# Longer contiguous runs for the weight loads, fewer K/V DMAs, and two alignment pads in a load-bound decode kernel

## Chip, cores, metric

One core of one Trainium2 chip. The metric is device time in microseconds of a whole launch. A profile's span is some 2 us shorter than the time of the same run, because it counts from the first instruction to the last. A run's state is "fast" or "slow" (over 1.5% above the fastest run of the same kernel); comparisons use fast runs alone.

## The reference

One token (B = S = 1) goes through a windowed attention over a cache and, in parallel, a squared-ReLU MLP. D = 512, 32 heads of 128, window W = 1024, F = 1376; everything is bf16.

```python
xn = layernorm(x)                                   # [1, 512]
q  = xn @ wq                                        # wq [512, 4096]
p  = softmax(q_h . K_h[3072:4096] / sqrt(128))      # per head, 1024 keys
o  = p @ V_h[3072:4096]                             # per head, 128
attn = concat(o) @ wo                               # wo [4096, 512]
mlp  = relu(xn @ w1 + b1)**2 @ w2 + b2              # w1 [512, 1376], w2 [1376, 512]
out  = x + attn + mlp
```

K and V are 8 MB each, wq and wo 4 MB each, w1 and w2 1.4 MB each: 28 MB are read once for very little arithmetic.

## The kernel before

All loads but three small rows (x and the two biases, which ACT issues) are issued by SP in one list, in the order in which they are used. The parts that the change touches (cuts are marked):

```python
plan = []
for kt in range(NKT):                                # wq: 4 DMAs, runs of 8192 B
    plan.append((wq_v[:, kt, :], A_wq[kt*128:(kt+1)*128, :], s_wq, ...))
plan.append((w1_sb, B_w1.rearrange("(k p) n -> p k n", p=128), s_w12, ...))       # runs of 2752 B
plan.append((w2_sb[:, 0:NJ-1, :], B_w2[0:1280].rearrange("(j p) n -> p j n", p=128), ...))  # 1024 B
plan.append((w2_sb[0:96, NJ-1, :], B_w2[1280:F, :], s_w12, ...))
for h in range(HQ):                                  # K: 32 DMAs of 256 KB, runs of 2048 B
    plan.append((k_sb[:, h, :], A_k_cache[0, h, S0:SK, :].rearrange("(p t) d -> p (t d)", p=128), kq[h//HPG], ...))
# ... V likewise, 32 DMAs ...
for g in range(NWO):                                 # wo: 8 DMAs, runs of 1024 B
    plan.append((wo_v[:, 4*g:4*g+4, :], A_wo[...].rearrange("(h d) n -> d h n", d=DH), woq[g], ...))
# PE, end of the kernel
for h in range(HQ):                                  # PV: 256 matmuls, one output column each
    if h % HPG == 0: pe.wait_ge(vq[h // HPG], 16 * HPG)
    # ... 8 matmuls into ot_ps[:, h]
pe.wait_ge(s_ot, 1)                                  # ACT has copied ot_ps to ot_sb
for h in range(HQ):                                  # 128 matmuls into four output columns
    if h % hpg == 0: pe.wait_ge(woq[h // hpg], 16)
    for c in range(4):
        pe.matmul(fin[c], lhsT=wo_v[:, h, c*128:(c+1)*128], rhs=ot_sb[:, h:h+1], ...)
# ... four copies, one transpose, one copy, output DMA
```

Buffers are laid out in SBUF in the order of their declaration. That put wbuf, which holds wq and later wo, 160 B past a multiple of 256 B in each partition, and w1 and w2 likewise.

## Time and profile before

| | before |
|---|---|
| time, median of 4 runs first, of 16 later | 80.44 us, 80.38 us |
| span of the profiled run | 78.2 us |
| DMA packets, bytes | 15,975, 28.1 MB |
| last wo load landed | 75.13 us |

The lines themselves are in the prediction. To read them: the GB/s row has forty slices of 1.96 us; the list of loads and the rates in the slices tell which load is running. "Packets" are what one of the 16 DMA engines moves at a time, one contiguous run each, and the small ones of 4 B are the semaphore writes that end each DMA (1,272 of them before, 16 for each of SP's 79 loads and a few more).

### The profile page before, as it was taken

The numbers are of one execution on the slowest core, as the hardware profiler recorded it, in microseconds if no ns is written. First come the engines' busy times: TensorE is split into PE (matmuls) and PEld (weight loads), VectorE is DVE, ScalarE is ACT, GpSimd is POOL, SyncE is SP. The second block draws the span as 40 slices with busy tenths as digits, with TensorE's granted clock in tenths as the row PEclk, the third lists the DMA queues.
The fourth block names the chain that finished last, engine by engine and source line by source line (L and its number), as shares of the span: only waits on it lengthen the run. The fifth ranks groups of instructions, "written<-read, shape, count | busy, mean of one in ns | idle before, by whom it ended". The sixth has DMA issues, their size and how long they took to land.

```text
span 78.2 us, 2026 instructions
## 1 busy us (share of the span) xinstructions
PE 50.0 (64%) x812; PEld 34.8 (45%) x812; DVE 26.0 (33%) x214; ACT 26.9 (34%) x33; POOL 2.2 (3%) x10
## 2 busy tenths in 40 slices
PE   0000102999296099999999999993398954850940
PEld 0000001358295094445554455371288954850920
DVE  0005500000103999899959990006300000000010
ACT  0501700242000049579999999900600000100011
POOL 7400000000000000000000000000000000000000
PEclk9999999999555555599999999999955555555555
DMA  2799999999999999999999999999999999999700
GB/s 34 285 404 423 431 427 398 400 362 347 368 399 402 405 407 404 400 404 407 401 401 406 406 404 398 410 398 404 402 409 404 395 375 354 350 349 349 233 15 1
DMA packets 15975, 28.12 MB, mean 359 GB/s; under 512 B 1275, under 2 KB 6749, under 8 KB 15454
## 3 DMA queue, kind: packets, MB, share of 16 engines
q1 hardware_dynamic: 15952, 27.99, 96.1%
q8 instruction: 6, 0.10, 0.5%
q14 instruction: 3, 0.02, 0.1%
q10 hardware_dynamic: 14, 0.01, 0.0%
HBM read 27.99 MB, written 0.00 MB: 358 GB/s over the span
## 4 chain that ended last, share of the span: by engine, by line
SPq 79%; DMA 11%; issue 5%; PE 1%; ACT 1%
SPq L227 79%; DMA wbuf<-in_A_wo_dram 11%; PE s_all L568 0%; PE stg L577 0%; ACT orow L301 0%; ACT col_bf L299 0%; PE f_ps L568 0%; PE a_ps L568 0%
## 5 line engine op out<-in xcount | busy, mean ns | idle before, releaser
L284 ACT ACTIVATE kt_sb<-stg 128x1024 bf16<-128x1024 bf16 x20 | 20.3, 1024 | 12.7 <-PE stg L501 11.8
L362 DVE SCALAR_TENSOR_TENSOR junk<-k_sb,qb_sb 128x128 bf16<-128x128 bf16 x96 | 20.6, 285 | 1.2 <-DMA k_sb<-in_A_k_cache_dram 1.2
L501 PE MATMUL stg<-identb,k_sb 128*128 128x128 bf16 x160 | 13.8, 240 | 2.6 <-DMA k_sb<-in_A_k_cache_dram 2.6
L501 PEld LDWEIGHTS stg<-identb,k_sb 128*128 128x128 bf16 x160 | 10.6, 108 | 10.7 <-ACT kt_sb L284 5.5
L508 PE MATMUL s_all<-kt_sb,qmask 128*32 128x512 bf16 x40 | 12.8, 408 | 0.1
L554 PE MATMUL b_ps<-pt_sb,v_sb 128*128 128x1 bf16 x256 | 7.1, 165 | 2.2 <-issue 1.8
L554 PEld LDWEIGHTS b_ps<-pt_sb,v_sb 128*128 128x128 bf16 x256 | 7.0, 104 | 2.4 <-issue 1.9
L362 DVE DVE_READ_ACCUMULATOR junk<-k_sb,qb_sb 128x1 f32 x96 | 7.8, 81 | 0.0
L419 PE MATMUL s_all<-wbuf,xb 128*128 128x512 bf16 x12 | 4.2, 521 | 4.4 <-DMA wbuf<-in_A_wq_dram 4.4
L403 DVE CAST col_bf<-a_ps 128x1 bf16<-128x1 f32 x1 | 0.2, 161 | 16.9 <-PE f_ps L568 16.9
L410 PE MATMUL a_ps<-identb,rows_a 1*128 1x1 bf16 x4 | 0.2, 160 | 8.6 <-DVE rows_a L327 8.6
L568 PE MATMUL a_ps<-ot_sb,wbuf 128*128 128x1 bf16 x32 | 3.6, 165 | 2.7 <-issue 2.7
L568 PEld LDWEIGHTS f_ps<-ot_sb,wbuf 128*128 128x128 bf16 x32 | 3.3, 104 | 2.8 <-issue 2.8
L568 PE MATMUL s_all<-ot_sb,wbuf 128*128 128x1 bf16 x64 | 3.8, 166 | 1.1 <-DMA wbuf<-in_A_wo_dram 0.8
L419 PEld LDWEIGHTS s_all<-wbuf,xb 128*128 128x128 bf16 x12 | 1.4, 126 | 6.8 <-DMA wbuf<-in_A_wq_dram 4.5
L296 ACT ACTIVATE ot_sb<-b_ps 128x32 bf16<-128x32 f32 x1 | 0.2, 198 | 11.9 <-PE b_ps L554 11.9
L274 ACT ACTIVATE qb_sb<-s_all 128x512 bf16<-128x512 f32 x3 | 1.8, 597 | 7.0 <-PE s_all L419 7.0
L443 PE MATMUL b_ps<-xncol,w_sb 128*128 128x1 bf16 (+1 forms) x44 | 3.1, 175 | 1.6 <-DMA w_sb<-in_B_w_dram 1.6
L568 PEld LDWEIGHTS s_all<-ot_sb,wbuf 128*128 128x128 bf16 x64 | 3.5, 105 | 1.4 <-DMA wbuf<-in_A_wo_dram 0.8
L410 PEld LDWEIGHTS a_ps<-identb,rows_a 1*128 1x128 bf16 x4 | 0.2, 100 | 8.5 <-issue 8.5
L337 DVE TENSOR_SCALAR qmask<-a_ps 128x4 bf16<-128x4 f32 x5 | 0.4, 167 | 10.0 <-PE a_ps L430 10.0
L568 PE MATMUL f_ps<-ot_sb,wbuf 128*128 128x1 bf16 x32 | 3.6, 165 | 0.0
(65 smaller groups left out, 37.9 us busy)
## 6 DMA issues: line engine op xcount, KB each, us to landing
k_sb<-in_A_k_cache_dram SPq DMA_DIRECT2D x32, 256.0 KB, 8.5
v_sb<-in_A_v_cache_dram SPq DMA_DIRECT2D x32, 256.0 KB, 8.5
wbuf<-in_A_wq_dram SPq DMA_DIRECT2D x4, 1024.0 KB, 8.0
wbuf<-in_A_wo_dram SPq DMA_DIRECT2D x8, 512.0 KB, 9.5
w_sb<-in_B_w_dram SPq DMA_DIRECT2D x1, 1376.0 KB, 13.9
w_sb<-in_B_w_dram SPq DMA_DIRECT2D x1, 1280.0 KB, 17.2
w_sb<-in_B_w_dram SPq DMA_DIRECT2D x1, 96.0 KB, 16.9
rows_a<-in_A_x_dram ACTq DMA_DIRECT2D x1, 1.0 KB
```

The source lines that it names most:

```text
L227: eng.dma_start(dst, srcap).then_inc(s_, 16)
L274: act.activation(out=qb_sb[:, c * 512 : (c + 1) * 512], in_=s_ps[c % NB_QB][:, :], func=ACT.Copy).then_inc(s_qbev, 1)
L284: act.activation(out=kt_sb[:, i % NS_KT, :], in_=stg_bf[i % NB_STG][:, :], func=ACT.Copy).then_inc(s_evA, 1)
L337: v.tensor_scalar(diag, qt_ps[:, h0 : h0 + 4], inv_sqrt_dh, None, op0=ALU.mult).then_inc(s_qmask, 1)
L362: v.scalar_tensor_tensor(out=junk[:, n % NJUNK, :], in0=k_sb[:, h, t * DH : (t + 1) * DH], scalar=inv_sqrt_dh, in1=qb_sb[:, (4 * ci + j) * ...
L410: ins = pe.matmul(xc_ps[:, kt : kt + 1], lhsT=xn_row[0:1, kt * 128 : (kt + 1) * 128], rhs=one11, start=True, stop=True)
L419: ins = pe.matmul(s_ps[c % NB_QB][:, :], lhsT=xb[:, kt, :], rhs=wq_v[:, kt, b * 512 : (b + 1) * 512], start=(kt == 0), stop=(kt == NKT - 1),)
L443: pe.matmul(ht_ps[0:msz, j : j + 1], lhsT=w1_sb[:, kt, j * 128 : j * 128 + msz], rhs=xncol[:, kt : kt + 1], start=(kt == 0), stop=False,)
L501: ins = pe.transpose(bank[:, t * 128 : (t + 1) * 128], k_sb[:, h, t * DH : (t + 1) * DH], identb[:, :])
L508: ins = pe.matmul(s_ps[c][0:32, :], lhsT=qmask[:, h, :], rhs=kt_sb[:, i % NS_KT, c * 512 : (c + 1) * 512], start=(first_op[c] == (idx, c)) ...
L554: ins = pe.matmul(ot_ps[:, h : h + 1], lhsT=v_sb[:, h, t * DH : (t + 1) * DH], rhs=pt_sb[:, t, h : h + 1], start=(t == 0), stop=(t == NT - 1),
L568: ins = pe.matmul(fin[c], lhsT=wo_v[:, h, c * 128 : (c + 1) * 128], rhs=ot_sb[:, h : h + 1], start=(DEBUG_ATTN_ONLY and h == 0), stop=(h = ...
```

## The change

Its intent is to make each contiguous run longer. A matrix of R rows over 128 partitions is loaded as "partition p takes rows p*k to p*k+k-1" instead of "partition p takes rows p, 128+p, ...", so that k rows are one run. What multiplies the matrix must then be ordered in the same way. For wq and w1 that is a stepped read of the normalised row; for w2 it is a stepped read of w1's columns (step of 10 elements); for wo the attention output, which has one head per column, must be rearranged, which the string of transposes, a permutation matmul and two copies does. K and V go out four heads per DMA. Two pads move the buffers.

```diff
+        pad_w = sb("pad_w", [128, 176], BF16)          # ahead of wbuf
+        pad_k = sb("pad_k", [128, 144], BF16)          # ahead of k_sb
-        for kt in range(NKT):
-            plan.append((wq_v[:, kt, :], A_wq[kt * 128 : (kt + 1) * 128, :], s_wq, ...))
+        plan.append((wbuf[:, :], A_wq.rearrange("(p k) n -> p (k n)", k=NKT), s_wq, ...))      # 32 KB runs
+        plan.append((w1_sb..., B_w1.rearrange("(p k) n -> p (k n)", k=NKT), s_w12, ...))       # 11008 B
+        plan.append((w2a_sb..., B_w2[0:1280].rearrange("(p a) n -> p (a n)", a=NA2), ...))     # 10 KB
+        plan.append((w2b_sb[:, :], B_w2[1280:F, :], s_w12, ...))
+        for g in range(NG):                                # K, V: four heads per DMA, runs still 2 KB
+            plan.append((k_sb[:, hs, :], A_k_cache[0, hs, S0:SK, :].rearrange("h (p t) d -> p h (t d)", p=128), kq[g], ...))
-  "(h d) n -> d h n"
+  wo_src = A_wo.rearrange("(p a) n -> p a n", a=32)        # 4 of 32 rows per DMA: 4 KB runs
     # ... FFN1
-    lhsT=w1_sb[:, kt, j * 128 : j * 128 + msz]
+    lhsT=w1_sb[:, kt, j : j + 10 * 127 + 1 : 10]           # j < 10
     # ... between PV and the wo product
+    for b4 in range(4):
+        pe.transpose(z_ps[rs, :], ot_sb[rs, :], identb[rs, rs], tile_position=(32 * b4, 32 * b4))
+    # VectorE: z_sb <- z_ps
+    pe.matmul(c_ps, lhsT=p4[:, :], rhs=z_sb[:, :], start=True, stop=True)
+    # VectorE: c_sb <- c_ps
-    rhs=ot_sb[:, h : h + 1]
+    rhs=c_sb[:, a : a + 1]
```

(Cut: semaphores, the building of the permutation p4 on GpSimd, the renamed w2 buffers.)

More of the change, by code (lines that the diff above doesn't have):

```diff
@@ L21 @@
 NJ = (F + 127) // 128
+NA2 = 10
+F2T = F - NA2 * 128
 NT = W // 128
@@ L34 @@
 HPG = HQ // NG
+KSEM = 16
 NWO = int(os.environ.get("KDEV_NWO", "8"))
@@ L94, in bass_parallel_sum__sliding_block_cached__dense_activation_squared_relu__decode_kernel @@
         xb = sb("xb", [128, NKT, 128], BF16)
+        pad_w = sb("pad_w", [128, 176], BF16)
         wbuf = sb("wbuf", [128, NKT * HQ * DH], BF16)
         w1_sb = sb("w1_sb", [128, NKT, F], BF16)
-        w2_sb = sb("w2_sb", [128, NJ, D], BF16)
+        w2a_sb = sb("w2a_sb", [128, NA2, D], BF16)
+        w2b_sb = sb("w2b_sb", [F2T, D], BF16)
+        p4 = sb("p4", [128, 128], BF16)
+        z_sb = sb("z_sb", [128, 32], BF16)
+        c_sb = sb("c_sb", [128, 32], BF16)
         hrelu = sb("hrelu", [128, NJ], F32)
@@ L117, in bass_parallel_sum__sliding_block_cached__dense_activation_squared_relu__decode_kernel @@
         wq_v = wbuf[:, :].rearrange("p (k n) -> p k n", k=NKT)
-        wo_v = wbuf[:, :].rearrange("p (h n) -> p h n", h=HQ)
+        wo_v = wbuf[:, :].rearrange("p (a n) -> p a n", a=32)
         one11 = identb[0:1, 0:1]
@@ L134, in bass_parallel_sum__sliding_block_cached__dense_activation_squared_relu__decode_kernel @@
         row4_ps = stg_bf[0][0:4, 256:384]
+        z_ps = stg_bf[1][:, 0:32]
+        c_ps = b_ps[:, 96:128]
         NB_QB = 2
@@ L175, in bass_parallel_sum__sliding_block_cached__dense_activation_squared_relu__decode_kernel @@
         s_colc = sem("s_colc")
+        s_p4 = sem("s_p4")
+        s_zt = sem("s_zt")
+        s_zsb = sem("s_zsb")
+        s_cps = sem("s_cps")
+        s_csb = sem("s_csb")
         s_row4 = sem("s_row4")
@@ L191, in bass_parallel_sum__sliding_block_cached__dense_activation_squared_relu__decode_kernel @@
         plan = []
-        for kt in range(NKT):
-            plan.append((wq_v[:, kt, :], A_wq[kt * 128 : (kt + 1) * 128, :], s_wq, 128 * 4096 * 2, False))
-        plan.append((w1_sb[:, :, :], B_w1.rearrange("(k p) n -> p k n", p=128), s_w12, D * F * 2, False))
-        plan.append((w2_sb[:, 0 : NJ - 1, :], B_w2[0 : (NJ - 1) * 128, :].rearrange("(j p) n -> p j n", p=128), s_w12, 1280 * D * 2, False))
-        plan.append((w2_sb[0 : F - (NJ - 1) * 128, NJ - 1, :], B_w2[(NJ - 1) * 128 : F, :], s_w12, 96 * D * 2, False))
-        for h in range(HQ):
-            plan.append((k_sb[:, h, :], A_k_cache[0, h, S0:SK, :].rearrange("(p t) d -> p (t d)", p=128), kq[h // HPG], W * DH * 2, False))
-        for h in range(HQ):
-            plan.append((v_sb[:, h, :], A_v_cache[0, h, S0:SK, :].rearrange("(p t) d -> p (t d)", p=128), vq[h // HPG], W * DH * 2, False))
-        hpg_ = HQ // NWO
+        plan.append((wbuf[:, :], A_wq.rearrange("(p k) n -> p (k n)", k=NKT), s_wq, D * HQ * DH * 2, False))
+        plan.append((w1_sb[:, :, :].rearrange("p k n -> p (k n)"), B_w1.rearrange("(p k) n -> p (k n)", k=NKT), s_w12, D * F * 2, False))
+        plan.append((w2a_sb[:, :, :].rearrange("p a n -> p (a n)"), B_w2[0 : NA2 * 128, :].rearrange("(p a) n -> p (a n)", a=NA2), s_w12, NA2 * 128 * D * 2, False))
+        plan.append((w2b_sb[:, :], B_w2[NA2 * 128 : F, :], s_w12, F2T * D * 2, False))
+        for g in range(NG):
+            hs = slice(g * HPG, (g + 1) * HPG)
+            plan.append(
+                (
+                    k_sb[:, hs, :],
+                    A_k_cache[0, hs, S0:SK, :].rearrange("h (p t) d -> p h (t d)", p=128),
+                    kq[g],
+                    HPG * W * DH * 2,
+                    False,
+                )
+            )
+        for g in range(NG):
+            hs = slice(g * HPG, (g + 1) * HPG)
+            plan.append(
+                (
+                    v_sb[:, hs, :],
+                    A_v_cache[0, hs, S0:SK, :].rearrange("h (p t) d -> p h (t d)", p=128),
+                    vq[g],
+                    HPG * W * DH * 2,
+                    False,
+                )
+            )
+        apg_ = 32 // NWO
+        wo_src = A_wo.rearrange("(p a) n -> p a n", a=32)
         for g in range(NWO):
@@ L204, in bass_parallel_sum__sliding_block_cached__dense_activation_squared_relu__decode_kernel @@
                 (
-                    wo_v[:, g * hpg_ : (g + 1) * hpg_, :],
-                    A_wo[g * hpg_ * DH : (g + 1) * hpg_ * DH, :].rearrange("(h d) n -> d h n", d=DH),
+                    wo_v[:, g * apg_ : (g + 1) * apg_, :].rearrange("p a n -> p (a n)"),
+                    wo_src[:, g * apg_ : (g + 1) * apg_, :].rearrange("p a n -> p (a n)"),
                     woq[g],
-                    hpg_ * DH * D * 2,
+                    apg_ * 128 * D * 2,
                     True,
@@ L258, in _ @@
                 ).then_inc(s_ident, 1)
+                g.memset(p4[:, :], 0.0).then_inc(s_pool, 1)
+                g.wait_ge(s_pool, 3)
+                p4v = p4[:, :].rearrange("q (a b) -> q a b", b=4)
+                g.affine_select(
+                    out=p4v,
+                    in_=p4v,
+                    compare_op=ALU.not_equal,
+                    fill=1.0,
+                    base=0,
+                    pattern=[[-1, 32], [-32, 4]],
+                    channel_multiplier=1,
+                ).then_inc(s_p4, 1)
             @block.scalar
@@ L353, in d_block @@
                     ci = dblk_index[b]
-                    v.wait_ge(kq[b], 16 * HPG)
+                    v.wait_ge(kq[b], KSEM)
                     v.wait_ge(s_qbev, ci + 1)
@@ L400, in _ @@
                 v.tensor_copy(pt_sb[:, :, :], pt_ps).then_inc(s_ptsb, 1)
+                v.wait_ge(s_zt, 1)
+                v.tensor_copy(z_sb[:, :], z_ps).then_inc(s_zsb, 1)
+                v.wait_ge(s_cps, 1)
+                v.tensor_copy(c_sb[:, :], c_ps).then_inc(s_csb, 1)
                 v.wait_ge(s_final, 1)
@@ L409, in _ @@
                 for kt in range(NKT):
-                    ins = pe.matmul(xc_ps[:, kt : kt + 1], lhsT=xn_row[0:1, kt * 128 : (kt + 1) * 128], rhs=one11, start=True, stop=True)
+                    ins = pe.matmul(xc_ps[:, kt : kt + 1], lhsT=xn_row[0:1, kt : kt + 4 * 127 + 1 : 4], rhs=one11, start=True, stop=True)
                 ins.then_inc(s_xc, 1)
-                pe.wait_ge(s_wq, 16 * NKT)
+                pe.wait_ge(s_wq, 16)
                 if NDB > 0:
@@ L440, in _ @@
                 for j in range(NJ):
-                    msz = min(128, F - j * 128)
+                    if j < NA2:
+                        msz = 128
+                        colsel = slice(j, j + NA2 * 127 + 1, NA2)
+                    else:
+                        msz = F2T
+                        colsel = slice(NA2 * 128, F)
                     for kt in range(NKT):
@@ L444, in _ @@
                             ht_ps[0:msz, j : j + 1],
-                            lhsT=w1_sb[:, kt, j * 128 : j * 128 + msz],
+                            lhsT=w1_sb[:, kt, colsel],
                             rhs=xncol[:, kt : kt + 1],
@@ L449, in _ @@
                         )
-                    ins = pe.matmul(ht_ps[0:msz, j : j + 1], lhsT=b1_row[0:1, j * 128 : j * 128 + msz], rhs=one11, start=False, stop=True)
+                    ins = pe.matmul(ht_ps[0:msz, j : j + 1], lhsT=b1_row[0:1, colsel], rhs=one11, start=False, stop=True)
                 ins.then_inc(s_ht, 1)
@@ L460, in emit_ffn2 @@
                             pe.matmul(fin[c], lhsT=b2_row[0:1, cs], rhs=one11, start=False, stop=False)
-                            for j in range(NJ):
-                                msz = min(128, F - j * 128)
-                                pe.matmul(fin[c], lhsT=w2_sb[0:msz, j, cs], rhs=hsq[0:msz, j : j + 1], start=False, stop=False)
+                            for j in range(NA2):
+                                pe.matmul(fin[c], lhsT=w2a_sb[:, j, cs], rhs=hsq[:, j : j + 1], start=False, stop=False)
+                            pe.matmul(fin[c], lhsT=w2b_sb[:, cs], rhs=hsq[0:F2T, NA2 : NA2 + 1], start=False, stop=False)
                 ops = []
@@ L494, in emit_tr @@
                     if g not in waited_k:
-                        pe.wait_ge(kq[g], 16 * HPG)
+                        pe.wait_ge(kq[g], KSEM)
                         waited_k.add(g)
@@ L551, in _ @@
                     if h % HPG == 0:
-                        pe.wait_ge(vq[h // HPG], 16 * HPG)
+                        pe.wait_ge(vq[h // HPG], KSEM)
                     for t in range(NT):
@@ L562, in _ @@
                 pe.wait_ge(s_ot, 1)
-                hpg = HQ // NWO
-                for h in range(HQ):
-                    if h % hpg == 0:
-                        pe.wait_ge(woq[h // hpg], 16)
+                for b4 in range(4):
+                    rs = slice(32 * b4, 32 * b4 + 32)
+                    ins = pe.transpose(z_ps[rs, :], ot_sb[rs, :], identb[rs, rs], tile_position=(32 * b4, 32 * b4))
+                ins.then_inc(s_zt, 1)
+                pe.wait_ge(s_zsb, 1)
+                pe.wait_ge(s_p4, 1)
+                pe.matmul(c_ps, lhsT=p4[:, :], rhs=z_sb[:, :], start=True, stop=True).then_inc(s_cps, 1)
+                pe.wait_ge(s_csb, 1)
+                apg = 32 // NWO
+                for a in range(32):
+                    if a % apg == 0:
+                        pe.wait_ge(woq[a // apg], 16)
                     for c in range(4):
@@ L569, in _ @@
                             fin[c],
-                            lhsT=wo_v[:, h, c * 128 : (c + 1) * 128],
-                            rhs=ot_sb[:, h : h + 1],
-                            start=(DEBUG_ATTN_ONLY and h == 0),
-                            stop=(h == HQ - 1),
+                            lhsT=wo_v[:, a, c * 128 : (c + 1) * 128],
+                            rhs=c_sb[:, a : a + 1],
+                            start=(DEBUG_ATTN_ONLY and a == 0),
+                            stop=(a == 31),
                         )
```

## The prediction

> **What bounds the kernel now.** I read the page's slices first, then its DMA queues, then the chain that ended last, then busy time by stage, then the timeline of PE near the end.
>
> The slices show the core's 16 DMA engines full from the second slice to the 37th, while no compute engine is full all the way:
>
> ```profile
> span 78.2 us, 2026 instructions
> DMA  2799999999999999999999999999999999999700
> GB/s 34 285 404 423 431 427 398 400 362 347 368 399 402 405 407 404 400 404 407 401 401 406 406 404 398 410 398 404 402 409 404 395 375 354 350 349 349 233 15 1
> q1 hardware_dynamic: 15952, 27.99, 96.1%
> q8 instruction: 6, 0.10, 0.5%
> by line: SPq L227 79.4%; DMA wbuf<-in_A_wo_dram 10.9%; issue 5.0%; PE s_all L568 0.5%; PE stg L577 0.4%; ACT orow L301 0.3%; ACT col_bf L299 0.3%; PE f_ps L568 0.2%; PE a_ps L568 0.1%
> 66.58 8.55 DMA wbuf<-in_A_wo_dram
> ```
>
> The chain is 79% the SP queue (L227 issues every load, and is held back by a full DMA queue) and then the last wo load, which lands at 66.58 + 8.55 = 75.13 us. Behind that only 16 matmuls, two copies, a transpose and the output remain, to 78.2. So the end is "last wo byte + 3.1 us". The bytes can't shrink (28 MB, each read once), so what counts is the rate, and the GB/s row shows that it isn't one rate. I cut windows in which one load alone runs (columns: window, us, busy PE, PEld, DVE, ACT, POOL, granted clock, DMA share, GB/s):
>
> ```profile
> 4.00:12.00 8.00, 0.24 (x4) 0.18 (x4) 2.13 (x7) 1.69 (x3) 0.00 (x0) 1.00 1.01 424
> 12.50:15.50 3.00, 2.28 (x6) 0.89 (x7) 0.00 (x0) 0.35 (x1) 0.00 (x0) 1.00 1.02 404
> 16.50:19.50 3.00, 2.89 (x85) 2.34 (x82) 0.07 (x1) 1.19 (x2) 0.00 (x0) 1.00 1.10 349
> 24.00:58.00 34.00, 28.56 (x274) 17.11 (x272) 22.88 (x199) 21.46 (x22) 0.00 (x0) 0.85 1.05 404
> 64.00:72.50 8.50, 3.92 (x136) 3.78 (x136) 0.00 (x0) 0.20 (x1) 0.00 (x0) 0.50 1.10 351
> ```
>
> By the kernel's order these are wq (contiguous runs of 8192 B), w1 (2752 B), w2 (1024 B), K and V (2048 B), wo (1024 B). The rate follows the length of the run, with equal busy share: a cost per packet. One packet takes size x 16 / rate on its engine: 8192 B 309 ns, 2752 B 109 ns, 2048 B 81 ns, 1024 B 47 ns. A line through the first two is 7.8 ns + 37.7 ns per KiB; it gives 83 and 45.5 for the other two, so it holds within 3%.
>
> PE is the second thing to look at, for it must not become the bound once the loads are quicker:
>
> ```profile
> 58.93 4.82 PE L554 MATMUL b_ps<-pt_sb,v_sb 128*128 128x1 bf16 x175 [0.39 <-DVE pt_sb L400]
> 65.56 2.32 PE L554 MATMUL b_ps<-pt_sb,v_sb 128*128 128x1 bf16 x81 [1.81 <-issue]
> 72.28 0.16 PE L568 MATMUL a_ps<-ot_sb,wbuf 128*128 128x1 bf16 x1 [2.73 <-issue]
> 75.18 0.21 PE L568 MATMUL s_all<-ot_sb,wbuf 128*128 128x1 bf16 x2 [0.77 <-DMA wbuf<-in_A_wo_dram]
> ```
>
> In its last 17 us PE waits only 0.8 us for wo. Its two longer halts (1.8 and 2.7 us) are "issue". Counted in the trace's list of PE records, weight loads and matmuls both, the halts stand at records 1217 and 1473: exactly 256 apart. Each comes beside one of the six "instruction" packets of 16 KB (at 63.0 and 69.7 us). PE ran out of instructions.
>
> **What the Trainium skill says.** (1) DMA: Bandwidth & Descriptors, section Why small descriptors are slow: each packet has a fixed cost inside the DMA engine. The trace agrees, with 7.8 ns by the line above. (2) The same page, How a descriptor splits into AXI transactions: one that starts off a 256 B boundary costs an extra transaction. The change's two pads put wbuf and w2 on such a boundary; 8 KB packets into the unaligned wbuf already fit the line, so I see no penalty and give the pads nothing. (3) Runtime: NRT & Kernel Launch, section Instruction fetch mechanics: instructions come in 16 KiB blocks of 256, fetched while the block before runs, and crossing is "mostly hidden". The block agrees with the 256 records; "hidden" doesn't, with 4.5 us of halts. (4) SBUF — State Buffer, its note on SBUF cachelines: reads that step to a new 16-byte line each time pay a penalty. No run yet shows it for a weight load; it matters for one rival.
>
> **The change part by part.** Per DMA engine (one sixteenth of the packets):
> - wq: 32 packets of 8 KB, 32 x 309 = 9.89 us, become 8 of 32 KB, 8 x (7.8 + 32 x 37.7) = 9.71. Saves 0.2.
> - w1: 32 x 109 = 3.49 become 8 of 11008 B, 8 x 413 = 3.30. Saves 0.2.
> - w2: 86 x 46.8 = 4.02 become 8 of 10 KB and 6 of 1 KB, 8 x 385 + 6 x 46.8 = 3.36. Saves 0.65.
> - wo: 256 x 46.8 = 11.98 become 64 of 4 KB, 64 x 158.6 = 10.15. Saves 1.85.
> - K and V stay 2 KB packets; 64 DMAs become 16. Each DMA ends in one 4-byte semaphore packet per engine, 9 ns each in the trace: at most 48 x 9 = 0.43, partly overlapped. Saves 0.3.
> - Sum 3.2 us, all on the path that ends last. The old sums, with K and V at 512 x 81 = 41.5, make 70.9, against 72.9 us from the first packet to the last, so the model accounts for 97%.
>
> Added, beside the loads: a memset and select on GpSimd (idle), four 32x32 transposes, a copy, one matmul, a copy between PV and the wo product. The kernel's own tail has such a string, copies 0.24, transpose 0.28, copy 0.27 with gaps, about 1.0 us from the last matmul on, so I take 1.2 us. Moved: w1's stationary operand is now read with a step of 10 elements; the counts of matmuls in both FFN products are the same.
>
> Loads alone: last wo at 71.9, end 3.2 us sooner, 77.2 us.
>
> Does PE keep up? The loads before K shrink by 1.05, so K comes 1.05 us sooner; ScalarE's evictions, which follow one another from 33.7 to 51.0 us, move with their start, so PV starts at 57.8 rather than 58.9. PV is 256 x 27.5 ns = 7.1 us, the copy 0.25, the new string 1.2, wo 128 x 27 ns = 3.5. Without halts that is 69.9, well ahead of 71.9. So the new string is free, if the halts don't grow.
>
> **The rivals.**
> (a) Instruction fetch becomes the bound. From crossing into a block to the arrival of the next but one took 5.4 us (60.2 to 65.56) and 6.7 us (65.56 to 72.28), while PE uses a block in 3.5. Moved to the new times with the same lags: 59.1 to 64.5, then 71.2, then the last 89 or so matmuls, 2.4 us: 73.6 against 75.7 before. Gain 2.1. For it: the halts are there now. Against: in the stretches of 2 KB packets two such fetches started 1.0 and 1.4 us after the crossing, against 2.8 and 4.1 us in and before the 1 KB stretch, so a queue of short packets seems to be what delays them, and that queue has a quarter of the packets now. With 2.4 us lags less, PE is back on the loads' path. K and V DMAs four times as large may delay a fetch more; that speaks for it.
> (b) The stepped w1 reads slow 44 weight loads of 105 ns. FFN1 ends at 24.7 and PE then waits for K until 27.2, so 2.5 us are free. Twice as long (4.6 us) would push the score stage by 2.1 us and PE's end to about 73 to 74: gain near 2. Three times would eat it all.
> (c) HBM doesn't like the new pattern: in the wo load, 128 rows at a pitch of 32 KB with 4 KB each; then wo stays near 350 GB/s and the gain is 1.4, 79.0 us. Nothing in the profile speaks for it, save that all loads before were one contiguous area per DMA or nearly so.
> (d) All is hidden: excluded, as the loads end the span.
>
> **Range and chances.** The loads' sum gives 77.2, (a) in part or (b) 78.3, (c) 79.0. I weigh the first at 0.6 and the others together at 0.4, and take 77.6. Below 76.5 the line would have to understate the gain by a quarter; above 79.0 two rivals must act together. 2% is 78.83. Faster 0.86, same 0.12, slower 0.02.
>
> **What would show it.** Right: GB/s in the wo stretch near 413 (4096 x 16 / 158.6), in w2's near 425, K and V 405 to 408; packets down from 15952 to about 10,000; last wo at about 72; PE waiting for wo at the end; the new string inside earlier idle time. Wrong: wo still near 350 (c); w1 weight loads over 150 ns and T-block transposes starting later than 27 us (b); PE halts of 2 us or more put down to "issue" right before the last wo matmuls, with no wait for wo (a). A time over 79.0 would mean the per-packet line is wrong or a wait took the loads' place; below 76.5 that alignment counts after all.

## The result

| | before | after |
|---|---|---|
| median, us | 80.38 (16 runs) | 77.33 (10 runs, two of them slow) |
| ratio of fast runs | | 0.9616 (95%: 0.9600 to 0.9631) |
| span, us | 78.2 | 75.2 |
| last wo load landed, us | 75.13 | 72.06 |

A ratio here is the mean time of one kernel's fast runs over the mean of the other's fast runs of the same rounds, so it isn't quite the ratio of the medians. The prediction was 77.6 us.

From the page of the changed kernel (clock granted to TensorE, DMA busy share, GB/s by slice of 1.88 us, packets):

```profile
span 75.2 us, 1991 instructions
PEclk9999999999985558999999999999995555555555
DMA  4698997999999999999999999999999999999500
GB/s 123 192 523 350 489 453 310 433 427 400 397 407 412 395 409 410 407 406 404 398 412 406 410 409 405 405 399 409 410 407 407 414 411 423 425 410 416 224 4 1
...
q1 hardware_dynamic: 10144, 27.99, 94.3%
```

The same bytes went in 10,144 packets instead of 15,952. The dips of the row of before, 347 to 368 in the w2 slices and about 350 in the last full ones, are gone. The jumps in slices 2 to 7 lie in the stretch of 32 KB packets, each of which lasts over 1.2 us; I take them for the booking of such a packet in one slice, as the sum is right.

Busy time by stage of the changed kernel (window, us, PE, PEld, DVE, ACT, POOL, clock, DMA share, GB/s), in this order: wq; w1; w2; K and V; wo.

```profile
4.00:12.00 8.00, 0.00 (x0) 0.00 (x0) 0.99 (x3) 0.15 (x1) 0.00 (x0) 1.00 0.96 414
12.50:15.00 2.50, 1.37 (x7) 0.64 (x8) 0.76 (x3) 1.06 (x2) 0.00 (x0) 1.00 1.00 427
15.80:18.40 2.60, 2.60 (x7) 0.88 (x6) 0.00 (x0) 1.18 (x2) 0.00 (x0) 1.00 1.02 433
24.00:55.00 31.00, 28.13 (x277) 17.53 (x276) 22.72 (x199) 21.41 (x22) 0.00 (x0) 0.92 1.05 406
62.50:69.50 7.00, 4.91 (x161) 4.54 (x162) 0.37 (x2) 0.20 (x1) 0.00 (x0) 0.50 1.03 418
```

The rate of wo went from 351 to 418 GB/s (413 was predicted), w2 from 349 to 433 (425 was predicted), w1 from 404 to 427; K and V moved from 404 to 406.

The chain that ended last (start, length, what) and the timeline of PE near the end, the lines with an idle time before them:

```profile
57.38 14.68 DMA wbuf<-in_A_wo_dram
```

```profile
56.27 4.83 PE L609 MATMUL b_ps<-pt_sb,v_sb 128*128 128x1 bf16 x175 [0.39 <-DVE pt_sb L446]
62.81 2.32 PE L609 MATMUL b_ps<-pt_sb,v_sb 128*128 128x1 bf16 x81 [1.71 <-issue]
65.41 0.21 PE L620 MATMUL stg<-identb,ot_sb 32*32 32x32 bf16 x4 [0.29 <-ACT ot_sb L342]
66.40 0.21 PE L631 MATMUL s_all<-c_sb,wbuf 128*128 128x1 bf16 x2 [0.29 <-DVE c_sb L450]
68.58 0.19 PE L631 MATMUL s_all<-c_sb,wbuf 128*128 128x1 bf16 x1 [0.93 <-issue]
72.11 0.21 PE L631 MATMUL s_all<-c_sb,wbuf 128*128 128x1 bf16 x2 [0.63 <-DMA wbuf<-in_A_wo_dram]
```

The end is still the last landing: PE waits for wo before its last 16 matmuls. The added string runs from 65.41 to 66.40, 1.0 us. The two halts for instructions are still there, again at the same record numbers 1217 and 1473 of PE's list (its semaphore records are counted too), 1.7 and 0.9 us long.

Three side effects lie upstream and didn't reach the end. The stepped read of w1 made the weight loads of FFN1 slower (one line's instructions; min/median/max ns, before and after), and the small row loads, which share the engines with 32 KB packets now, held up the layer norm (a line of the waits of the changed kernel; 6.5 us before):

```profile
L443 PEld LDWEIGHTS b_ps<-xncol,w_sb x44: 103/105/198, 21.0 to 24.3; 128*128 128x128 bf16 x40, 128*96 128x96 bf16 x4
```

```profile
L498 PEld LDWEIGHTS b_ps<-xncol,w_sb x44: 135/157/195, 20.8 to 25.7; 128*128 128x128 bf16 x40, 128*96 128x96 bf16 x4
DVE stat_t L365 <- DMA rows_c<-in_B_b_dram: 10.8, 1, 10.8
```

The 105 ns before were measured at half the granted clock, at which all of FFN1 ran there. At the full clock a read without a step took 95 to 98 ns (the run with w2 by single rows, below); the stepped one took 157 in the median at either clock.

And ScalarE's 20 evictions of transposed keys ran without a gap from 27.24 us on, where they had two gaps, 0.8 and 0.6 us, before (ScalarE's timeline, first kernel then second):

```profile
28.39 2.85 ACT L284 ACTIVATE kt_sb<-stg 128x1024 bf16<-128x1024 bf16 x3 [10.35 <-PE stg L501]
32.04 1.02 ACT L284 ACTIVATE kt_sb<-stg 128x1024 bf16<-128x1024 bf16 x1 [0.79 <-PE stg L501]
33.69 17.35 ACT L284 ACTIVATE kt_sb<-stg 128x1024 bf16<-128x1024 bf16 x16 [0.63 <-PE stg L501]
```

```profile
27.24 21.25 ACT L330 ACTIVATE kt_sb<-stg 128x1024 bf16<-128x1024 bf16 x20 [7.63 <-PE stg L556]
```

So PV began 2.7 us sooner (56.27, from 58.93). The granted clock goes with it: by the trace's clock records it was at half from 19.6 to 33.2 us before, over the first transposes, and only from 22.1 to 28.9 us after. That gain isn't steady, and isn't on the path: with the added string twice and with other wo groups (below) PV began at 57.4 and 57.5, and the time was no longer.

### The profile page after: what moved, and what is told of

Read it like the earlier page. It is cut to its first block, busy times and chain, and to the rows that moved or that the text cites. A ratio compares the mean times of both kernels' runs of the same rounds, so it can differ in the third digit from the quotient of the medians.

```text
span 75.2 us, 1991 instructions
## 1 busy us (share of the span) xinstructions
PE 51.3 (68%) x817; PEld 36.3 (48%) x817; DVE 26.2 (35%) x216; ACT 26.9 (36%) x33; POOL 2.9 (4%) x12
## 3 DMA queue, kind: packets, MB, share of 16 engines
q1 hardware_dynamic: 10144, 27.99, 94.3%
## 4 chain that ended last, share of the span: by engine, by line
SPq 74%; DMA 20%; issue 2%; PE 1%; ACT 1%
SPq L261 74%; DMA wbuf<-in_A_wo_dram 20%; PE s_all L631 0%; PE stg L640 0%; ACT orow L347 0%; ACT col_bf L345 0%; PE f_ps L631 0%; PE a_ps L631 0%
## 5 line engine op out<-in xcount | busy, mean ns | idle before, releaser
L563 PE MATMUL s_all<-kt_sb,qmask 128*32 128x512 bf16 x40 | 11.9, 384 | 0.1
L469 PE MATMUL s_all<-wbuf,xb 128*128 128x512 bf16 x12 | 5.1, 612 | 0.8 <-DVE xb L377 0.8
L631 PE MATMUL s_all<-c_sb,wbuf 128*128 128x1 bf16 x64 | 3.9, 167 | 2.5 <-DMA wbuf<-in_A_wo_dram 1.3
L631 PEld LDWEIGHTS s_all<-c_sb,wbuf 128*128 128x128 bf16 x64 | 3.6, 105 | 2.8 <-DMA wbuf<-in_A_wo_dram 1.4
L365 DVE BATCH_NORM_STATS2 stat_t<-rows_a 1x6 f32<-1x512 bf16 x1 | 0.7, 682 | 10.8 <-DMA rows_c<-in_B_b_dram 10.8
L498 PE MATMUL b_ps<-xncol,w_sb 128*128 128x1 bf16 (+1 forms) x44 | 4.4, 204 | 0.0
L631 PE MATMUL a_ps<-c_sb,wbuf 128*128 128x1 bf16 x32 | 3.7, 165 | 0.0
L631 PE MATMUL f_ps<-c_sb,wbuf 128*128 128x1 bf16 x32 | 3.7, 165 | 0.0
L563 PEld LDWEIGHTS s_all<-kt_sb,qmask 128*32 128x32 bf16 x40 | 2.3, 95 | 2.8 <-ACT kt_sb L330 0.6
L498 PEld LDWEIGHTS b_ps<-xncol,w_sb 128*128 128x128 bf16 (+1 forms) x44 | 3.5, 155 | 0.1
```

Source lines behind the costliest of these rows:

```text
L365: chain(v.bn_stats(st6, x_row))
L469: ins = pe.matmul(s_ps[c % NB_QB][:, :], lhsT=xb[:, kt, :], rhs=wq_v[:, kt, b * 512 : (b + 1) * 512], start=(kt == 0), stop=(kt == NKT - 1),)
L498: pe.matmul(ht_ps[0:msz, j : j + 1], lhsT=w1_sb[:, kt, colsel], rhs=xncol[:, kt : kt + 1], start=(kt == 0), stop=False,)
L563: ins = pe.matmul(s_ps[c][0:32, :], lhsT=qmask[:, h, :], rhs=kt_sb[:, i % NS_KT, c * 512 : (c + 1) * 512], start=(first_op[c] == (idx, c)) ...
L631: ins = pe.matmul(fin[c], lhsT=wo_v[:, a, c * 128 : (c + 1) * 128], rhs=c_sb[:, a : a + 1], start=(DEBUG_ATTN_ONLY and a == 0), stop=(a == ...
```

## The experiments

The question was not whether the time fell but which part of the change made it fall: the length of the runs, the number of DMAs, or the pads; and how near PE is. All kernels passed the comparison with the reference, and so did the one that is wrong: by the inputs' scales the attention term is tiny beside x, so the comparison hardly tests the order of wo. (By hand: the string puts o[h, 32b + i] at row 32b + h, column i; p4 picks row 32 (p mod 4) + p div 4 for partition p, which is head p div 4 and thus element 32 p + i of the flat output. That is the order of the new wo load.) Each call ran on one chip together with runs of the kernel before.

### wo part alone

Edit, on the kernel before: the wo hunk and the added string, nothing else; the new small buffers are declared last, so no other buffer moves.

> The kernel before with the wo part alone (wo by rows of four, 4 KB packets, and the added string of transposes and copies; wbuf stays off the 256 B boundary). Per-packet line (my theory): 64 x 158.6 instead of 256 x 46.8 ns per DMA engine, 1.85 us less by the line, 1.6 us by what the wo stretch of the changed kernel took (61.7 to 71.7 against 63.05 to 74.65): ratio to before 0.977 to 0.980, wo packets of 159 ns. Rival, that PE's instruction halts set the end: the halts of 1.8 and 2.7 us stay where they are, PV cannot start sooner than 58.9, and the end moves by less than 1.2 us, ratio 0.985 or more. Rival, that alignment makes the gain: wo packets longer than 159 ns and a gain well under 1.6.

Measured: 78.70 us, ratio 0.9789 (0.9775 to 0.9804), 1.7 us less. The wo stretch ran at 415 GB/s (same columns as above):

```profile
64.00:71.00 7.00, 3.99 (x127) 3.62 (x127) 0.37 (x2) 0.20 (x1) 0.00 (x0) 0.50 1.03 415
```

This fits the line and contradicts the rival of the halts: PV began at 58.6 as before, yet the end moved by the whole 1.7. By the trace's packet records the packets were 159 ns in the median, 161.2 on the mean, into a buffer off the boundary.

### wo part undone

```diff
-    wo by rows of four, 4 KB runs; string; rhs=c_sb[:, a:a+1]
+    wo as before, 1 KB runs; no string; rhs=ot_sb[:, h:h+1]     # everything else as changed, pads too
```

> The changed kernel with the wo part undone (1 KB packets, but into a wbuf that the pad has put on a 256 B boundary; no added string). Per-packet line: 1.6 to 1.85 us over the changed kernel, ratio to before 0.98 to 0.985, wo packets of 46 to 51 ns as before. If alignment counts, 1 KB packets become shorter here than the 49 ns of before[...], and less than 1.2 us is lost.

Measured: 78.24 us, ratio 0.9725 (0.9703 to 0.9747): 0.9 us over the changed kernel, not 1.6 to 1.85. My expectation failed and its second half held: the same part is worth 1.7 us without the pads and 0.9 with them. (The profiled run was a slow one, so its K and V rates are not used; its wo packets took 46.3 ns on the mean against 49.8 before.) So alignment, to which the prediction gave nothing, had to be measured by itself.

### Only the pads

```diff
+        pad_w = sb("pad_w", [128, 176], BF16)      # on the kernel before, ahead of wbuf
+        pad_k = sb("pad_k", [128, 80], BF16)       # ahead of k_sb, so that K and V stay aligned
```

> The kernel before with nothing but two pads (352 B ahead of wbuf, 160 B ahead of k_sb), so that wbuf, w1 and w2 start on a 256 B boundary like K and V already did. My prediction gave alignment nothing: ratio 1.00. Revised theory after the run with wo undone, where 1 KB packets into an aligned wbuf took 46.3 ns on the mean against 49.8: wo 256 x 3.5 = 0.9 us and w2 86 x 4.8 = 0.4 us per DMA engine, 1.0 to 1.3 us less, ratio 0.984 to 0.988; 1 KB packets of 46 ns in both stretches, 2 KB packets unchanged at 84.

Measured: 78.90 us, ratio 0.9803 (0.9784 to 0.9822): 1.6 us less for 512 unused bytes per partition. The stretches of 1 KB packets, w2 and then wo, ran at 386 and 382 GB/s, against 349 and 351:

```profile
16.50:19.20 2.70, 2.70 (x80) 2.23 (x79) 0.00 (x0) 1.19 (x2) 0.00 (x0) 1.00 1.09 386
64.00:71.50 7.50, 4.70 (x165) 4.48 (x163) 0.00 (x0) 0.20 (x1) 0.00 (x0) 0.50 1.09 382
```

The sum of the packets answers for it: from the trace's packet records, mean ns,

| kernel | w2 | wo | K, V (2 KB) | w1 (2752 B) |
|---|---|---|---|---|
| before | 51.1 (1 KB) | 49.8 (1 KB) | 84.6 | 111.5 |
| only the pads | 46.0 (1 KB) | 46.3 (1 KB) | 84.3 | 109.0 |
| changed | 385 (10 KB) | 160.0 (4 KB) | 84.3 | 413 (11008 B) |
| changed, no pads | 385 (10 KB) | 163.4 (4 KB) | 89.1 | 413 (11008 B) |

256 x 3.5 + 86 x 5.1 + 512 x 0.3 + 32 x 2.5 ns = 0.90 + 0.44 + 0.15 + 0.08 = 1.6 us per DMA engine.

The cost isn't one sum per packet. Off the boundary, packets of 1 to 4 KB lasted 1.2 to 5.1 ns longer (here and in the runs with 4 KB and 2 KB packets off it), but longer packets show nothing: wq's 8 KB packets had a median of 309 ns before and with the pads, and w1's and w2's of 11008 B and 10 KB took 413 and 385 ns with the pads and without. Why it stops there stays open.

### No pads

```diff
-        pad_w = sb("pad_w", [128, 176], BF16)      # on the changed kernel
-        pad_k = sb("pad_k", [128, 144], BF16)
```

> The changed kernel without its two pads, so that wbuf, w1, w2 and also K and V land off a 256 B boundary. My theory gives alignment nothing: the same time as the changed kernel within 0.2 us, 2 KB packets of 84 ns. Rival, each packet pays one more transaction: 2 KB packets rise from 84 to about 93 ns[...], 512 packets per DMA engine make 4 us more, the whole gain gone.

Measured: 80.11 us, ratio 0.9958 (0.9933 to 0.9984): the change without its pads gains almost nothing. My expectation of "the same within 0.2 us" failed: it was 2.8 us more. The rival had the direction, but its 9 ns per 2 KB packet was twice what was measured (89.1 against 84.3). The reason is not only wbuf. The new small buffers shift K and V to 128 B past a multiple of 256 B, and their rate falls to 386 GB/s:

```profile
24.00:58.00 34.00, 29.20 (x296) 18.12 (x297) 23.09 (x200) 21.44 (x22) 0.00 (x0) 0.85 1.05 386
```

### K and V alone off the boundary

```diff
-        pad_k = sb("pad_k", [128, 144], BF16)      # on the changed kernel
+        pad_k = sb("pad_k", [128, 80], BF16)
```

> The changed kernel with the second pad 128 B shorter, so that K and V alone start 128 B past a 256 B boundary; wbuf, w1 and w2 stay aligned. Theory: nearly all of the 2.8 us that were lost without both pads comes from K and V: 2 KB packets of 88 to 89 ns instead of 84, 512 x 4.8 = 2.5 us, ratio to before 0.990 to 0.996. Rival, the loss lay in wq, w1, w2 and wo: ratio 0.962 as the changed kernel, packets of 84.

Measured: 79.54 us, ratio 0.9885 (0.9859 to 0.9911), 2.2 of the 2.8 us; packets 88.8 ns on the mean.

```profile
24.00:58.00 34.00, 29.85 (x311) 18.75 (x312) 23.08 (x200) 21.46 (x22) 0.00 (x0) 0.85 1.05 386
```

A 2 KB packet pays 4.5 ns, 512 of them 2.3 us. Of the other 0.6 us lost without pads, wo's 64 packets at 3.4 ns give 0.2; the rest isn't found.

The second state is a rival here, since a kernel's state is judged against its own fastest run, and the packets alone don't rule it out: in the slow run of the kernel with the wo part undone, K and V were aligned and their packets took 88.2 ns on the mean all the same. What speaks against chance is the count. All eight runs of the two kernels with K and V off the boundary were like this, within 0.5 us in each kernel, but only 5 of the 46 runs of the changed kernel and its variants with aligned K and V were slow. Whether the two share a mechanism stays open. The 1 KB packets are free of this rival: in that slow run they took 46.3 ns, as in the fast run with only the pads.

Two starts were tried, 160 B and 128 B past the boundary. That 256 B are enough and 512 aren't needed follows from w1 and w2: w2 lies right behind w1, which is 43 x 256 B long, so only one of the two can start on a multiple of 512 B, and with the pads neither pays (109.0 and 46.0 ns).

### K and V one head per DMA

```diff
+        for h in range(HQ): plan.append((k_sb[:, h, :], ...))   # and V; waits for 4 x 16 again
```

> The changed kernel with K and V issued one head per DMA again (64 DMAs instead of 16; same packets of 2 KB). Semaphore packets, my theory: 48 more of them per DMA engine at up to 9 ns each, 0.3 us over the changed kernel (0.25 to 0.43), ratio to before 0.965. Rival, a fixed cost of issuing: SP is held back by a full queue anyway, so 48 more issues of 0.5 us would show only if the queue ran dry; then over 1 us. Rival, nothing: 0.

Measured: 77.55 us, ratio 0.9650 (0.9619 to 0.9681). That is 0.2 to 0.3 us over the changed kernel, where 0.3 was expected, but the interval is as wide; a cost over 0.7 us for the 48 DMAs is excluded, zero is not.

### The added string twice

```diff
+    # after c_sb: four transposes, z_sb copy, matmul with p4, c_sb copy once more
```

> The changed kernel with the added string (four 32x32 transposes, copy, matmul, copy) made twice, one after the other. My prediction: the string lies in time that PE has left before the last wo lands, so the second one costs nothing: ratio 0.962 as the changed kernel, within 0.1 us, and the halt at the next block of instructions shrinks or the waits for wo do. Rival, the string is on the path: 1.0 us more (65.41 to 66.40 in the changed kernel), ratio 0.974.

Measured: 77.20 us, ratio 0.9598 (0.9567 to 0.9628): no cost. PE's timeline shows where it went: wo's matmuls begin at 68.42 instead of 66.40, and the halt for instructions after them shrinks from 0.93 to 0.24. (Of these 2.0 us the second string is 1.0; the rest is PV, which began 1.1 us later in this run.)

```profile
66.44 0.21 PE L624 MATMUL stg<-identb,ot_sb 32*32 32x32 bf16 x4 [0.29 <-ACT ot_sb L342]
67.43 0.21 PE L632 MATMUL stg<-identb,ot_sb 32*32 32x32 bf16 x4 [0.28 <-DVE c_sb L450]
68.42 0.21 PE L642 MATMUL s_all<-c_sb,wbuf 128*128 128x1 bf16 x2 [0.28 <-DVE c_sb L454]
69.78 0.21 PE L642 MATMUL s_all<-c_sb,wbuf 128*128 128x1 bf16 x2 [0.24 <-issue]
```

### Two wo groups never loaded

```diff
-        for g in range(NWO):                        # loads of wo
+        for g in range(NWO - 2):
-                            lhsT=wo_v[:, a, ...]    # 128 matmuls stay
+                            lhsT=wo_v[:, a % 24, ...]
```

The result is wrong. How much of 2.5 us of removed load shows tells how far the loads are ahead of everything else.

> The changed kernel with two of the eight wo groups never loaded (their matmuls read the first groups again: a wrong result, on purpose; all 128 matmuls stay). Loads alone bound the end: 2 x 1.27 = 2.5 us less than the changed kernel, about 74.8 us, ratio 0.930. PE and its instruction halts stand close behind: in the changed kernel the last halt ends at 68.6 and 89 matmuls of 27 ns would end at 71.0 without waits against 72.7 measured, so only about 1.7 us are to be had, 75.6 us, ratio 0.940, and no wait for wo before the last matmuls.

Measured: 76.65 us, ratio 0.9504 (0.9464 to 0.9543), one run slow, and that the profiled one: 0.9 us less than the changed kernel, short of both expectations. Run once more for a profile:

> Again the kernel with two wo groups never loaded, because its profile fell in a slow run (K and V packets of 87 ns). In a fast run I expect the last wo landing near 69.2 us and the last wo matmuls after an instruction halt that ends at 68.5 or later, without a wait for wo of more than 0.3 us: PE bounds it. If instead a wait for wo still stands before the last matmuls, loads bound it and the 0.9 us is a puzzle.

Measured: 76.27 us, ratio 0.9483 (two fast runs), about 1.1 us less. The last wo landed at 69.35, and PE's timeline shows no wait for wo after the last halt:

```profile
63.57 2.32 PE L609 MATMUL b_ps<-pt_sb,v_sb 128*128 128x1 bf16 x81 [1.74 <-issue]
69.35 0.19 PE L631 MATMUL s_all<-c_sb,wbuf 128*128 128x1 bf16 x1 [0.93 <-issue]
72.15 0.27 PE L640 MATMUL stg<-identb,col_bf 128*4 128x128 bf16 x1 [0.33 <-ACT col_bf L345]
```

Here PE bounds it. The next bound stands about 1 us behind the loads, nearer than the 1.7 us that I worked out from the changed kernel's profile alone, because in this run PV began at 57.0 and not at 56.3, and the halts follow its start.

### w2 by single rows

```diff
-    w2a: "(p a) n -> p (a n)", 10 KB runs;  w1 columns with a step of 10
+    w2a: "(a p) n -> p a n", 1 KB runs, aligned;  w1 columns side by side
```

> The changed kernel with w2 loaded by single rows of 1 KB again, aligned, so that w1's columns are read without a step. Per-packet line: 86 x 46.3 instead of 8 x 385 + 6 x 46.3 ns, 0.6 us more than the changed kernel, ratio 0.968 to 0.970. Weight loads of FFN1 back from 157 to 105 ns and FFN1 from 5.2 to 3.8 us: if the stepped read had cost time at the end (my rival b), that comes back here and the kernel is not slower, ratio 0.962 or less; if it is hidden, the whole 0.6 shows.

Measured: 77.55 us, ratio 0.9645 (0.9605 to 0.9684), beside 77.35 us and 0.9621 for the changed kernel in the same rounds: 0.2 us more. The weight loads of FFN1 came down to 97 ns in the median (about 105 where the clock was at half). The cost is between my two expectations and the intervals overlap, so the times decide nothing: neither 0 nor the whole 0.6 is excluded. That the stepped read doesn't show at the end rests on the changed kernel's trace, in which PE still waits 0.63 us for wo.

### Six wo groups of unequal size

```diff
-    wo in eight DMAs of 4 rows per partition
+    WOG = [8, 8, 8, 4, 2, 2]
```

> An attempt at a better kernel: the changed kernel with wo in six groups of 8, 8, 8, 4, 2 and 2 rows per partition instead of eight of 4. Per-packet line (8.7 ns + 37.6 per KiB): 24 packets of 8 KB, 8 of 4 KB, 16 of 2 KB per DMA engine, 10.02 us instead of 10.18, and 8 matmuls instead of 16 behind the last landing, 0.2 us: 0.35 us less than the changed kernel, 77.0 us. If PE's halts are as close behind the loads as the run without two wo groups says (0.9 us to be had by taking away 2.5 us of loads), some of that is lost: 0.1 to 0.35. Slower only if an 8 KB packet holds up the instruction fetch.

> The changed kernel itself, on the same chip and in the same rounds as the three below, as their measure: 77.3 us, ratio 0.960 to 0.963 in its fast runs.

Measured: 77.07 us, ratio 0.9591 (0.9550 to 0.9633), beside the changed kernel's 77.35 us and 0.9621 (0.9575 to 0.9666) on the same chip. That is 0.3 us the right way and below what these rounds can separate. The wait for wo before the last matmuls fell from 0.63 to 0.18 us:

```profile
72.24 0.22 PE L631 MATMUL s_all<-c_sb,wbuf 128*128 128x1 bf16 x2 [0.18 <-DMA wbuf<-in_A_wo_dram]
```

## Why the prediction was right, and where it wasn't

**The bound was read rightly.** The loads ended the span before and after; the last landing moved by 3.07 us and the time by 3.05. The prediction's sum was 3.2.

**The per-packet line was nearly right, for a reason partly wrong.** It foresaw 158.6, 385, 413 and 1214 ns for packets of 4 KB, 10 KB, 11008 B and 32 KB; the medians are 159, 385, 413 and 1213. But it credited all of the old short packets' slowness to their length. Half was alignment. By the runs (each against the kernel before), the 3.1 us divide so: pads alone 1.6; wo's long runs on top of aligned buffers 0.9 (0.9725 less 0.9616, of 80.4 us); the rest, that is wq, w1, w2 and the grouping of K and V, 0.6 by difference, not tested part by part.

**The step that failed** is "I see no penalty and give the pads nothing". Its evidence was circular: the 8 KB packets "already fit the line" because the line was drawn through them and through w1's, both unaligned. Packets of 8 KB in truth pay nothing that shows (above); the error was to carry this over to the short ones. The fit "within 3%" hid it. It compared times worked out from rates, as if the busy shares were equal, but they run from 1.01 to 1.10, so packets overlap and last longer than the rate says: 84.6 ns for 2 KB, not 81, and 49.8 to 51.1 for 1 KB, not 47. These records lie up to 12% over the line's 45.5, and were there to be read. A line through aligned packets alone is 8.7 ns + 37.6 ns per KiB. That the sum came out right is partly luck: the old times had the misalignment in them, and the line for the new packets had next to none of it, since long packets don't pay; where packets would have paid, in K and V above all, the pads kept it away. Had the change come without pads, the same working would have said 77.6, and 80.1 was measured.

**wq** was to save 0.2 us; its last packet ended at 12.83 us against 12.75, and at 12.64 in a second profile of the changed kernel, so no saving is shown.

**K and V** were to save 0.3 by fewer semaphore packets; measured 0.2 to 0.3, not separable from zero.

**The string** was called free; the run with two of them shows it. It lies in time in which PE would otherwise wait for instructions.

**Rival (a), instruction fetch,** didn't bind, but not for the reason given. I held the queue of short packets for the cause of late fetches. In the changed kernel no such queue is left at the end, and crossing to arrival still took 5.3 and 5.8 us (57.5 to 62.8, 62.8 to 68.6; 5.4 and 6.7 before). It stayed behind the loads because PE reached the first of these crossings at 57.5 us instead of the 59.1 that I had worked out, and the second lag was 0.9 us shorter than before. It is close: with six wo groups PV began 1.2 us later than in the changed kernel's profile, and PE still waited for wo, but only 0.18 us. (The block that is late is the next one, 256 records on, and not "the next but one" as the prediction has it.) What delays a fetch for so long stays open.

**Rival (b), the stepped read,** happened at half the size: 157 ns instead of 105, FFN1 5.3 us long instead of 3.8 (20.8 to 26.2). With the late layer norm it used up all of PE's wait for K, 2.6 us; the transposes still began sooner, at 26.2 us instead of 27.35. **Rival (c), the pitch of 32 KB,** didn't happen: 418 GB/s.

## What to carry to other kernels

In a kernel bound by loads, sort the stretches of the GB/s row by the length of the contiguous runs and by the start address of each destination before deciding what a rate is due to, and read the packets' own durations beside the rates; the cheapest thing to try, a pad, gave half the gain here. Adding small buffers ahead of large ones can cost more than a layout change wins, so print the addresses and pad again whenever a buffer is added. Then ask what stands right behind the loads: here it is PE's instruction stream, about 1 us away.

## What the Trainium skill lacked or had wrong

- DMA: Bandwidth & Descriptors, How a descriptor splits into AXI transactions, tells of a descriptor that starts off 256 B, in terms of reads. The runs show the cost for the destination's address in SBUF: 1 KB packets 49.8 to 51.1 ns at 160 B past the boundary and 46 on it, 2 KB packets 88.8 against 84.3 at 128 B past it, and nothing for packets of 8 KB and more; 2.2 us of 80 when K and V alone were off. The section Rules for kernel authors has no rule on the start address of a destination.
- The same page, Rules for kernel authors, asks for 1 MiB or more per DMA. With the queue always full, 1 MB instead of 256 KB per DMA for K and V was worth 0.2 to 0.3 us in 77, which isn't separable from nothing (over 0.7 is excluded); the length of the run and its alignment decided.
- Runtime: NRT & Kernel Launch, Instruction fetch mechanics, calls the crossing of a 16 KiB block "mostly hidden". PE used a block of 256 records in 3.4 us, the next one took 5.3 to 6.7 us to arrive beside full DMA engines, and PE halted for 0.9 to 2.7 us at the last two crossings of both kernels.
- SBUF — State Buffer, the note on cachelines, gives no size for weight loads. A step of 20 B raised a 128-column weight load from 105 ns (half clock) or 96 ns (full clock) to 157 ns at either.
